# A retention layer and a rational feed-forward network in one kernel: fewer steps per weight, one transfer of constants, another opening order, and loads held back four deep

## The chip, the cores and the metric

The kernel runs on one core of a Trainium2 chip. The core has five engines with queues of their own: TensorE (PE in the rows, with PEld for its weight loads), VectorE (DVE), ScalarE (ACT), GpSimd (POOL) and SyncE (SP), which here only issues transfers. The metric is the device time of one execution in microseconds: the median of three runs.

## The reference

```python
# attention: 8 batches x 8 heads, 576 tokens, 64 dimensions a head
scores = q @ k^T / sqrt(64)
gamma  = 1 - 2 ** (-5 - head)
ret    = scores * where(i >= j, gamma ** (i - j), 0)
x      = (ret @ v), heads side by side          # 4608 tokens x 512
# feed-forward with a rational activation
h = x @ w_in                                    # 512 -> 2048
P = a0 + a1*h + a2*h^2 + a3*h^3
Q = 1 + |b0|*|h| + |b1|*h^2
out = (P / (Q + 1e-6)) @ w_out                  # 2048 -> 512
```

`w_in` and `w_out` come to the kernel as 64-bit floats and are turned into 32-bit ones on the chip.

## The kernel before

**Work.** The 4608 tokens are 36 units of 128. A unit brings two transfers of 512 KB, `qk` (q and k) and `kv` (k and v in another layout). The first eight units are handled by `attention`: q is scaled (`scale_q`), v is scaled (`scale_v`), PE makes the scores in `ps`, DVE masks them (`decay`), PE multiplies by v and adds to the state (`outputs`), PE adds what older tokens give through the state `S_sb` (`cross`), ACT and DVE split the result into `xhi` and `xlo` (`keep_hi`, `keep_lo`), DVE adds to the state (`grow`) and POOL fades it (`fade`). `ps` has two buffers, so the scores of a unit wait until the unit two places before has left its buffer; `cross` of a unit waits for `fade` of the one before. Later units go through `late_visit`, whose work lies between the steps of the feed-forward network.

**Feed-forward.** The tokens are 9 blocks of 512; each block has 16 steps, one for each 128 of the 2048 hidden columns. A step is `gemm1` (12 matmuls into `h`: high times high, high times low, low times high), a chain of elementwise work on ACT, DVE and POOL that leaves `g`, and `gemm2` (12 matmuls into `acc`). The first 24 steps are "early": they keep work in the PSUM bank of `h`.

**Weights.** Each of 32 weight tiles (512 KB of 64-bit words, `bits`) is turned into two 32-bit parts `w`. ACT takes the upper word without its sign (`begin`, tile `c`) and the next digits of the lower word (`digit`, tile `t`), DVE joins them by a shift and an or (`join`), DVE puts the sign back (`sign`), ACT rounds to the high part (`high_part`), POOL or DVE subtracts for the low part (`low_part`).

**What sets the order.** `Plan` holds every task with a due time and a cost, walks a clock of its own and writes each engine's instructions in the order in which it picks them; the engines then run strictly in that order and wait for each other by semaphores. `DUE`, `FIRST`, `HOLD`, `LAG`, `BACK`, `SLACK` and `LOADS` are the tables that steer it. `LOADS` lists the first transfers in order ("0" is a unit, "w0" a weight). All transfers are issued by SP. Their semaphores are eight, used in turn, so a transfer waits for the landing of the one eight places ahead.

**Start.** PE runs eight matmuls on zeros (`WARM`, into `unread`), then waits for the first scaled q.

Every instruction of a task passes through one wrapper, so nearly all rows of the profile carry its line (L71); the tiles tell them apart.

Of the kernel before, what the change touches and what calls it, by code (L numbers as in the profile page):

```python
# [34 lines left out]
V_POOL = range(4)  # L35
IN_BANK = 24
WARM = 8
AHEAD = -6
REACH = 7.4
FIRST = (-30.37, -29.34, -25.59, -24.33, -24.08, -16.98, -16.13, -17.66)  # L40
UNITS = (20.48, 2.58, -2.5)
LATE = {'scale': -1.0, 'decay': 0.201, 'middle': 0.3, 'grow': 0.524, 'fade': 0.6, 'keep_hi': 0.3, 'keep_lo': 0.5}
LEAD = -2.2
CNV = 3
CNT = 1
SHIFT = 60
LOADS = 'w0 0 gq mask 1 w1 gv 2 w2 3 w4 w5 w3 5 4 ab w7 6 w9 w6 w10 w8 7 w11'.split()
# [6 lines left out]
LAG = {'PE': 0.25, 'ACT': 0.097, 'DVE': 0.217, 'POOL': 0.16, 'SP': 0}  # L54
BACK = {'PE': 0.281, 'ACT': 0.157, 'DVE': 0.06, 'POOL': 0.097, 'SP': 0.015}
DUE = {'p_begin': 0.5, 'size': 0.727, 'p_mul': 0.7, 'p_mul2': 0.93, 'v_line': 0.797, 'v_mul': 0.806, 'log': 1.578, 'exp': 1.838, 'quot': 1.6, 'check': 1.65, 'better': 0.79, 'g_hi': 1.888, 'g_lo': 2.167, 'gemm2': 3.44, 'begin': -0.243, 'digit': 0.045, 'join': 0.128, 'sign': -0.303, 'high_part': 1.252, 'low_part': 0.8, 'scale_q': -0.354, 'scale_v': -0.5, 'scores': 0.178, 'decay': 0.311, 'outputs': 1.268, 'cross': 0.51, 'keep_hi': 1.415, 'keep_lo': 0.942, 'grow': 0.669, 'fade': 0.87}
HOLD = {('POOL', 'scale_v'): 3.0, ('DVE', 'p_begin'): 0.616, ('DVE', 'high_part'): 0.5, ('DVE', 'g_hi'): 1.221, ('DVE', 'keep_hi'): 1.153, ('DVE', 'g_lo'): 99.0, ('DVE', 'low_part'): 1.002, ('POOL', 'v_mul'): 0.229}
SLACK = {'PE': 0.19, 'ACT': 0.283, 'DVE': 0.2, 'POOL': 0.006, 'SP': 0.301}

ADJ = {}  # L60


class InOrder:
# [5 lines left out]
    def __getattr__(self, name):  # L69
        method = getattr(self.engine, name)  # L70
        return lambda *a, **k: self.tc.keep_in_program_order(method(*a, **k))  # L71

# [28 lines left out]
class Plan:  # L101
# [19 lines left out]
    def run(self):  # L121
# [14 lines left out]
        dma, left, now, reach = 0.0, len(self.tasks), -2.0, REACH  # L136
        while left:
            best = None
            for e, queue in wait.items():
                found = []  # L140
                for t in queue:
                    if e != "SP" and t.due > now + reach:
                        continue
                    names = [r for r, _ in t.takes]
                    ready = [self.rings[r].ready(names[:j].count(r)) for j, r in enumerate(names)]
                    if None in ready:
                        continue
                    _, _, shared, hold = t.ways[e]
                    s = max([0.0, *ready, *(a.end - BACK[e] * (a.engine == e) for a in t.after)]) + hold
                    s = max(s, clock[e])  # L150
                    if shared:
                        s = max(s, port["POOL" if e == "DVE" else "DVE"])
                    found.append((s, t.due, t))
# [21 lines left out]
            if e == "SP":  # L175
                clock["SP"] = s + 0.43
                dma = max(dma, s + 1.4) + cost
                t.end = dma + 1.0
# [15 lines left out]
def retention_ffn(ctx: ExitStack, tc: tile.TileContext, qk, kv, w_in, w_out, ab, masks, masks2, gq, gv, out):  # L194
# [8 lines left out]
    cnt = ctx.enter_context(tc.tile_pool(name="cnt", bufs=CNT))  # L203
# [9 lines left out]
    pe, act, dve, pool, sp = (InOrder(tc, e) for e in (nc.tensor, nc.scalar, nc.vector, nc.gpsimd, nc.sync))  # L213
# [3 lines left out]
        "qk": 2, "kv": 2, "xp": 2, "cnv": CNV, "t": CNT, "v": 2, "u": 2, "p": 3, "g": 3, "o0": 1, "o1": 1,  # L217
# [40 lines left out]
    bits, parts, joins = {}, {}, []  # L258
# [3 lines left out]
    def weight(order, s, w, f, loaded):  # L262
# [11 lines left out]
        def digit():  # L274
# [3 lines left out]
        def join():  # L278
# [20 lines left out]
        def low_part_v():  # L299
# [3 lines left out]
        t = add("ACT", d + DUE["begin"], 0.55, begin, [loaded], [("cnv", k)])  # L303
        t = add("ACT", d + DUE["digit"], 0.55, digit, [t], [("t", k)])
        t = add("DVE", d + DUE["join"], 0.61, join, [t], [], [("t", k)], True)
        joins.append(t)
        t = add("DVE", d + DUE["sign"], 0.61, sign, [t], shared=True)
        hi = add("ACT", d + DUE["high_part"], 0.53, high_part, [t], other=[("DVE", 0.5, high_part_v, True)])
        w_ready[k] = hi, add(
            "POOL", d + DUE["low_part"], 1.21, low_part, [hi], [], [("cnv", k)], True, [("DVE", 0.61, low_part_v, True)]  # L310
# [20 lines left out]
    def load_unit(n, due, after=()):  # L331
# [4 lines left out]
        def of(w, nm):  # L336
# [12 lines left out]
            add("SP", due + 0.01 * w, 524 / 390.0, of(w, nm), after, [] if late else [(nm, n)])  # L349
# [9 lines left out]
    def scale(n, at_, got, consts):  # L359
        def scale_q():  # L360
            q, _ = qk_of(n)
            pool.tensor_tensor(q, q, gq_sb, ALU.mult)

        def scale_v(by=dve):
            _, v = kv_of(n)
            dec = gv_sb[:, (n >= EARLY) * H : (n >= EARLY) * H + H].unsqueeze(2).broadcast_to([P, H, D])
            by.tensor_tensor(v, v, dec, ALU.mult)

        def scale_v_p():
            scale_v(pool)  # L370

        tq = add("POOL", at_(DUE["scale_q"]), 1.21, scale_q, [got[0], consts["gq"]], shared=True)
        tv = add("DVE", at_(DUE["scale_v"]), 0.6, scale_v, [got[1], consts["gv"]], shared=True,
                 other=[("POOL", 1.21, scale_v_p, True)])
        return tq, tv

    def attention(n, d, gap, got, consts, prev):
# [121 lines left out]
        th = add("ACT", at_(DUE["keep_hi"]), 0.5, keep_hi, done, [("xp", b)] if n % 4 == 0 else [], gives,  # L499
# [27 lines left out]
    def visit(n):  # L527
        m, heads = n + 1, [(j, g) for j in range(2) for g in range(NPAIR)]
        if "ps" not in late_s:
# [5 lines left out]
        if m < NU:  # L535
            bank["s"] = ps_h.tile([P, 512], F32, tag="h", name=f"ps{n}")
# [15 lines left out]
        if n >= EARLY:  # L552
# [17 lines left out]
    def decay(n):  # L570
        scr[n] = cnv.tile([P, 2, NPAIR, D], F32, tag="c", name=f"s{n}")
# [52 lines left out]
    def late_visit(n, d, got, consts, prev, hold):  # L624

        old, m = n >= EARLY, n + 1
        new, u = m < NU, (n + 1) % 9
        tq = tv = None
        if new:
            dn = d + LATE["scale"]  # L630
            tq = add("POOL", dn, 1.21, lambda: pool.tensor_tensor(qk_of(m)[0], qk_of(m)[0], gq_sb, ALU.mult),
# [7 lines left out]
            def scale_v_p():  # L639
# [3 lines left out]
                     other=[("POOL", 1.21, scale_v_p, True)])  # L643
        key = f"ps{n}"
        tm = te = None
        if m in sooner:
            tm = add("DVE", d - 1.5, 0.42, named(middle, m), [prev["visit"], prev.get("fade")])
        if n + 2 in sooner:
# [36 lines left out]
        if tm is None:  # L685
            tm = add("DVE", d + LATE["middle"], 0.42, named(middle, m), [ts, prev.get("fade"), *hold])
        tg = tf = None
        if u not in (4, 8):
            first = S_of[m + 1] == "S1" and "S1" not in S_of[: m + 1]
            tg = add("DVE", d + LATE["grow"], 0.42, named(grow, m), [tm, ts, *(joins if first else [])],  # L690
                     [("t", "S1")] if first else [])
        if u != 8:
            tf = add("POOL", d + LATE["fade"], 0.57, named(fade, m), [tg or tm], shared=True)
# [7 lines left out]
    def feed_forward(i, b, f, begins, ends):  # L701
        key = b, f
        early = i < IN_BANK
# [19 lines left out]
        def p_begin():  # L723
            e = els[key] = {"p": el3.tile([P, 512], F32, tag="p", name=f"p{nm}")}
            act.activation(e["p"], hs[key], AF.Identity, bias=a2, scale=a3)

        def p_begin_v():
            e = els[key] = {"p": el3.tile([P, 512], F32, tag="p", name=f"p{nm}")}
            dve.tensor_scalar(e["p"], hs[key], a3, a2, ALU.mult, ALU.add)
# [7 lines left out]
        def p_mul():  # L737
            p = els[key]["p"]
            dve.tensor_tensor(p, p, hs[key], ALU.mult)
# [279 lines left out]
```

## Time and profile before

| | |
|---|---|
| median of 3 runs | 899.9 us (898.13 to 900.02) |
| the profiled execution | 900.45 us, its span 898.6 us |
| PE busy | 882.8 us, 98% of the span |
| DVE, ACT, POOL busy | 790.4, 653.2, 163.7 us |
| transfers | 67.41 MB, 66.28 MB of them on SP's queue |
| chain that ended last | PE 92% |

PE is busy for all but 16 us of the span. In the table the busy times say how much of the span an engine worked, not that it was the bound; where PE waits, and for what, is in the rows below.

### The profile page before, as it was taken

How to read it: one execution, taken by the hardware profiler on the slowest of the kernel's cores; microseconds unless marked ns; L12 is line 12 of the kernel's file. 1: busy time of each engine (PE TensorE's matmuls, PEld its weight loads, DVE VectorE, ACT ScalarE, POOL GpSimd, SP SyncE). 2: the span in 40 equal slices, each digit the busy share in tenths (PEclk: the TensorE clock that was granted, in tenths of full speed). 3: DMA queues.
4: the chain of work that ended last, by engine and by line, in shares of the span. 5: the costliest groups of instructions: out<-in, count | busy, mean ns of one | idle time of the engine just before them, and what ended most of it. 6: DMA issues, size and time to landing. Idle time of an engine off the chain costs nothing.

```text
span 898.6 us, 17725 instructions
## 1 busy us (share of the span) xinstructions
PE 882.8 (98%) x7344; PEld 730.3 (81%) x7344; DVE 790.4 (88%) x1215; ACT 653.2 (73%) x1019; POOL 163.7 (18%) x141
## 2 busy tenths in 40 slices
PE   6999999999999999999999999999999999999998
PEld 5777888887888888888888888888888888888886
DVE  4899999988999888988989888988888888987976
ACT  3589999965667767666766677767676786767765
POOL 3565664522211100011101110001100001000000
PEclk9999999999999999999999999999999999999999
DMA  9991000033311112111211131112211021001001
GB/s 357 407 406 69 1 1 1 0 112 123 109 49 61 58 34 70 41 47 60 95 48 48 59 107 48 48 47 74 80 48 47 26 74 44 1 1 47 1 1 47
DMA packets 22641, 67.41 MB, mean 75 GB/s; under 512 B 2592, under 2 KB 4512, under 8 KB 22560
## 3 DMA queue, kind: packets, MB, share of 16 engines
q1 hardware_dynamic: 22560, 66.28, 20.6%
q8 instruction: 57, 0.93, 0.4%
q14 instruction: 24, 0.20, 0.1%
HBM read 56.83 MB, written 9.44 MB: 74 GB/s over the span
## 4 chain that ended last, share of the span: by engine, by line
PE 92%; DVE 3%; DMA 3%; issue 0%; SPq 0%; ACT 0%; POOL 0%; ACTq 0%; DVEq 0%; POOLq 0%
PE acc L71 42%; PE h L71 42%; PE ps L71 7%; DMA bits<-in_w_in 2%; DVE p L71 1%; DMA kv<-in_kv 1%; SPq L71 0%; DVE c L71 0%; DVE s L71 0%; DVE kv L71 0%; DVE xlo L71 0%; DVE v L71 0%; ACT xhi L71 0%; ACT o L71 0%; DVE g L71 0%
## 5 line engine op out<-in xcount | busy, mean ns | idle before, releaser
L71 PE MATMUL acc<-w,g 128*128 128x512 f32 x1632 | 394.2, 390 | 0.0
L71 PEld LDWEIGHTS acc<-w,g 128*128 128x128 f32 x1632 | 305.5, 188 | 64.2 <-POOL w L71 0.4
L71 PE MATMUL h<-xhi,w 128*128 128x512 f32 x1152 | 310.6, 392 | 0.8 <-DVE p L71 0.7
L71 PEld LDWEIGHTS h<-xhi,w 128*128 128x128 f32 x1152 | 213.9, 188 | 47.4 <-DVE p L71 2.1
L71 ACT ACTIVATE p<-h,ab_sb 128x512 f32<-128x512 f32 x143 | 110.8, 775 | 90.7 <-PE h L71 88.5
L71 PE MATMUL h<-xlo,w 128*128 128x512 f32 x576 | 154.2, 390 | 0.0
L71 DVE TENSOR_TENSOR p<-p,h 128x512 f32<-128x512 f32 x144 | 98.4, 683 | 53.8 <-ACT u L71 50.9
L71 DVE SCALAR_TENSOR_TENSOR p<-p,ab_sb,h 128x512 f32<-128x512 f32 x168 | 124.5, 744 | 10.6 <-ACT u L71 8.0
L71 PEld LDWEIGHTS h<-xlo,w 128*128 128x128 f32 x576 | 108.1, 188 | 23.0
L71 ACT ACTIVATE g<-p 128x512 fp32r<-128x512 f32 x136 | 85.6, 629 | 46.5 <-DVE p L71 44.3
L71 ACT ACTIVATE u<-v,qc 128x512 f32<-128x512 f32 x120 | 86.7, 723 | 44.4 <-DVE v L71 44.4
L71 ACT ACTIVATE v<-u,absb 128x512 f32<-128x512 f32 x124 | 101.1, 815 | 3.6
L71 DVE SCALAR_TENSOR_TENSOR p<-p,ab_sb,u 128x512 f32<-128x512 f32 x120 | 95.7, 798 | 4.3 <-ACT u L71 4.3
L71 ACT ACTIVATE u<-h 128x512 f32<-128x512 f32 x144 | 84.8, 589 | 10.5 <-DVE v L71 5.7
L71 DVE SCALAR_TENSOR_TENSOR p<-v,p 128x512 f32<-128x512 f32 x120 | 86.4, 720 | 3.9
L71 DVE TENSOR_TENSOR v<-v,u 128x512 f32<-128x512 f32 x120 | 83.1, 693 | 4.3 <-ACT v L71 3.2
L71 DVE SCALAR_TENSOR_TENSOR v<-v,u 128x512 f32<-128x512 f32 x120 | 84.6, 705 | 0.0
L71 DVE TENSOR_TENSOR g<-p,g 128x512 fp32r<-128x512 f32 x112 | 77.3, 690 | 3.8 <-ACT g L71 2.9
L71 ACT ACTIVATE u<-u 128x512 f32<-128x512 f32 x120 | 75.0, 625 | 2.1
L71 POOL TENSOR_TENSOR qk<-qk,gq_sb 128x512 f32<-128x512 f32 x36 | 49.4, 1374 | 84.6 <-DMA qk<-in_qk 75.9
L71 PEld LDWEIGHTS ps<-qk 64*64 64x64 f32 (+1 forms) x1024 | 38.0, 146 | 18.8 <-issue 10.4
L71 POOL TENSOR_TENSOR S_sb<-S_sb,gv_sb 128x256 f32<-128x256 f32 x18 | 15.7, 872 | 191.7 <-DVE S_sb L71 190.0
(58 smaller groups left out, 766.3 us busy)
## 6 DMA issues: line engine op xcount, KB each, us to landing
qk<-in_qk SPq DMA_DIRECT2D x36, 512.0 KB, 3.9
kv<-in_kv SPq DMA_DIRECT2D x36, 512.0 KB, 5.2
bits<-in_w_in SPq DMA_DIRECT2D x16, 512.0 KB, 10.1
bits<-in_w_out SPq DMA_DIRECT2D x16, 512.0 KB, 10.2
out<-o SPq DMA_DIRECT2D x14, 512.0 KB, 3.3
out<-o SPq DMA_DIRECT2D x8, 256.0 KB, 2.3
x<-in_kv SPq DMA_DIRECT2D x7, 256.0 KB, 5.1
gq_sb<-in_gq SPq DMA_DIRECT2D x1, 256.0 KB, 6.5
```

Source lines behind the costliest of these rows:

```text
L71: return lambda *a, **k: self.tc.keep_in_program_order(method(*a, **k))
```

## The change

- `begin` now uses the parametric rectifier in place of the absolute value: positive words keep their scale, negative ones are multiplied by minus 2 to the 32, which sets the bit that `join`'s shift moves to the sign's place. `sign` goes. `begin` and `digit` write in place in `bits`, so tile `t` goes, and `join` writes `c`.
- Four constants (`gq`, `gv`, the second mask, `ab`) come in one tile `fac`, 301 KB, in the first transfer; the second mask is no longer loaded later.
- In early steps three additions of a per-partition constant move from ACT to DVE instructions that were there anyway (`p_begin` to `p_mul`, `v_line` to `v_mul`), and the logarithm's bias is a number in the instruction.
- `v_mul` runs on POOL in nine steps (0 to 5, 10, 11, 17) instead of four.
- The planner's tables are new: load order, due times of the early steps (`DUE`; later steps keep the old ones as `STEADY`), costs, holds; `scale_q` may go to DVE. It also knows the rule below.
- Each transfer from the fifth to the 46th waits for the landing of the one four places ahead (`Loads`). There are eleven warm-up matmuls instead of eight.
- `late_visit` can now also serve units below eight (`DENSE`, `VISITS`); with `DENSE = 8` it doesn't.

```diff
-WARM = 8
+WARM = 11
-LOADS = 'w0 0 gq mask 1 w1 gv 2 w2 3 w4 w5 w3 5 4 ab w7 6 w9 w6 w10 w8 7 w11'.split()
+LOADS = 'gq 0 mask 1 0v 2 1v 2v 3 w0 5 3v 5v w2 w1 w5 4 w4 6 w3 w6 4v w9 w7 w11 w10 7v 7 6v w8'.split()
+OUTSTANDING = 8
+THROTTLE = 4
+THROTTLED = 46
...
+class Loads(InOrder):
+    def dma_start(self, *a, **k):
+        new = self.tc.keep_in_program_order(self.engine.dma_start(*a, **k))
+        if THROTTLE <= len(self.begun) < THROTTLED:
+            after = mybir.DependencyInfo(mybir.DependencyClass.Sync, mybir.DependencyReason.DATA)
+            self.tc.add_manual_dep(new.ins, self.begun[-THROTTLE].ins.name, after, reason="few loads at a time")
+        self.begun.append(new)
+        return new
...
         def begin():
-            c_[0] = cnv.tile([P, DM], I32, tag="c", name=f"c{nm}")
-            act.activation(c_[0].bitcast(F32), words()[1].bitcast(F32), AF.Abs, scale=math.ldexp(1.0, -112))
+            x = words()[1].bitcast(F32)
+            act.activation(x, x, AF.Prelu, scale=math.ldexp(1.0, -112), alpha=-math.ldexp(1.0, 32))
 
         def digit():
-            c_[1] = cnt.tile([P, DM], I32, tag="t", name=f"t{nm}")
-            act.activation(c_[1], words()[2], AF.Copy, scale=15 * 2.0**-17)
+            act.activation(words()[0], words()[2], AF.Copy, scale=15 * 2.0**-17)
 
         def join():
-            dve.scalar_tensor_tensor(c_[0], c_[0], 3, c_[1], ALU.logical_shift_left, ALU.bitwise_or)
-
-        def sign():
-            dve.scalar_tensor_tensor(c_[0], words()[1], -0x80000000, c_[0], ALU.bitwise_and, ALU.bitwise_or)
+            c_[0] = cnv.tile([P, DM], I32, tag="c", name=f"c{nm}")
+            dve.scalar_tensor_tensor(c_[0], words()[1], 3, words()[0], ALU.logical_shift_left, ALU.bitwise_or)
...
-            act.activation(e["p"], hs[key], AF.Identity, bias=a2, scale=a3)
+            if early:
+                act.activation(e["p"], hs[key], AF.Copy, scale=a3)
+            else:
+                act.activation(e["p"], hs[key], AF.Identity, bias=a2, scale=a3)
...
-            act.activation(e["r"], e["v"], AF.Ln, bias=qc)
+            act.activation(e["r"], e["v"], AF.Ln, bias=QC)
```

SP's queue at its start, before. `qk` and `kv` carry the unit's number, `bits0_f` is tile f of `w_in`.

```order
L71 DMA bits0_0_117<-in_w_in 128x512
L71 DMA qk0_119<-in_qk 128x1024
L71 DMA kv0_121<-in_kv 128x1024
L71 DMA gq_sb_101<-in_gq 128x512
L71 DMA mask_sb_98<-in_masks 128x320
L71 DMA qk1_125<-in_qk 128x1024
L71 DMA kv1_127<-in_kv 128x1024
L71 DMA bits0_1_129<-in_w_in 128x512
L71 DMA gv_sb_100<-in_gv 128x20
```

The same place in the change:

```order
L90 DMA fac_99<-in_factors 128x602
L90 DMA qk0_116<-in_qk 128x1024
L90 DMA mask_sb_98<-in_masks 128x320
L90 DMA qk1_119<-in_qk 128x1024
L90 DMA kv0_122<-in_kv 128x1024
L90 DMA qk2_124<-in_qk 128x1024
L90 DMA kv1_127<-in_kv 128x1024
L90 DMA kv2_138<-in_kv 128x1024
L90 DMA qk3_143<-in_qk 128x1024
L90 DMA bits0_0_171<-in_w_in 128x512
```

Constants and `qk0` are now the first two; the first weight goes from place 1 to 10; `kv1` stays at place 7.

DVE's queue at its start, before (`s` is the masked scores, `S_sb` the state, `kv0<-kv0` the scaling of v):

```order
L71 SCALAR_TENSOR_TENSOR c0_0_132<-c0_0_132,t0_0_136 128x512
L71 SCALAR_TENSOR_TENSOR c0_0_132<-bits0_0_117,c0_0_132 128x512
L71 TENSOR_TENSOR w0_0_152<-c0_0_132,w0_0_152 128x512
L71 TENSOR_TENSOR s0_179<-ps0_164,mask_sb_98 128x1024
L71 TENSOR_TENSOR kv0_121<-kv0_121,gv_sb_100 128x512
L71 TENSOR_TENSOR kv1_127<-kv1_127,gv_sb_100 128x512
L71 TENSOR_TENSOR s1_226<-ps1_183,mask_sb_98 128x1024
L71 COPY S_sb_105<-ps0_164 128x256
L71 TENSOR_TENSOR kv2_138<-kv2_138,gv_sb_100 128x512
L71 TENSOR_TENSOR xlo0_252<-ps0_164,xhi0_251 128x4x128
L71 SCALAR_TENSOR_TENSOR c0_1_198<-c0_1_198,t0_1_205 128x512
L71 SCALAR_TENSOR_TENSOR c0_1_198<-bits0_1_129,c0_1_198 128x512
```

The same place in the change:

```order
L79 TENSOR_TENSOR s0_140<-ps0_129,mask_sb_98 128x1024
L79 TENSOR_TENSOR kv0_122<-kv0_122,fac_99 128x512
L79 TENSOR_TENSOR s1_174<-ps1_145,mask_sb_98 128x1024
L79 TENSOR_TENSOR kv1_127<-kv1_127,fac_99 128x512
L79 COPY S_sb_101<-ps0_129 128x256
L79 TENSOR_TENSOR xlo0_180<-ps0_129,xhi0_179 128x4x128
L79 TENSOR_TENSOR kv2_138<-kv2_138,fac_99 128x512
L79 TENSOR_TENSOR S_sb_101<-S_sb_101,ps1_145 128x256
L79 TENSOR_TENSOR xlo0_180<-ps1_145,xhi0_179 128x4x128
L79 TENSOR_TENSOR s2_232<-ps2_215,mask_sb_98 128x1024
L79 SCALAR_TENSOR_TENSOR c0_0_243<-bits0_0_171 128x512
```

The weights' work has moved behind the attention of units 0 and 1, and is one instruction a weight instead of two.

PE's queue between the first units and the first `gemm1` (`h0_0`), in the change:

```order
L79 MATMUL ps1_145<-qk1_119,S_sb_101 64x128 x8
L79 MATMUL ps2_215<-qk2_124 128x128 x8
L79 MATMUL ps3_234<-qk3_143 128x128 x8
L79 MATMUL ps2_215<-s2_232,kv2_138 64x128 x8
L79 MATMUL ps2_215<-kv2_138 64x64 x8
L79 MATMUL ps2_215<-qk2_124,S_sb_101 64x128 x8
L79 MATMUL ps3_234<-s3_263,kv3_200 64x128 x8
L79 MATMUL ps3_234<-kv3_200 64x64 x8
L79 MATMUL ps3_234<-qk3_143,S_sb_101 64x128 x8
L79 MATMUL ps5_325<-qk5_176 128x128 x8
L79 MATMUL h0_0_348<-xhi0_179,w0_0_266 128x512 x4
```

Before, the same eleven rows stand there in the same order; PE's queue differs up to here only in the three added warm-up matmuls.

## Rows read from the trace of the kernel before

**Rows 1.** Windows: stretch, length, busy (instructions) by engine, clock, DMA share, GB/s

```profile
0.00:30.86 30.86, 21.03 (x272) 19.12 (x272) 18.18 (x26) 11.48 (x18) 11.69 (x14) 1.00 0.96 370
30.86:62.00 31.14, 30.38 (x312) 24.41 (x311) 28.98 (x43) 22.43 (x39) 17.43 (x17) 1.00 1.03 407
62.00:112.00 50.00, 49.91 (x219) 40.35 (x218) 48.57 (x76) 49.63 (x86) 29.69 (x23) 1.00 0.19 75
112.00:894.40 782.40, 781.52 (x6547) 646.41 (x6545) 694.62 (x1073) 568.69 (x879) 104.90 (x89) 1.00 0.15 49
894.40:898.60 4.20, 0.00 (x0) 0.00 (x0) 0.00 (x0) 0.92 (x2) 0.00 (x0) 0.80 0.65 246
```

**Rows 2.** Timeline of PE, 0 to 31 us: start, duration, what, idle before

```profile
1.06 3.78 PE L71 MATMUL unread<-S_sb 128*128 128x128 f32 x16 [1.06 <-DVE qc L71]
10.04 3.79 PE L71 MATMUL ps<-qk 64*128 64x128 f32 x32 [5.20 <-POOL qk L71]
...
16.48 1.04 PE L71 MATMUL ps<-s,kv 128*64 128x128 f32 x16
17.36 0.63 PE L71 MATMUL ps<-kv 128*64 128x64 f32 x16
18.88 1.09 PE L71 MATMUL ps<-qk,S_sb 64*64 64x128 f32 x16 [0.89 <-POOL S_sb L71]
19.90 1.16 PE L71 MATMUL ps<-qk 64*128 64x128 f32 x16
...
30.86 1.20 PE L71 MATMUL h<-xhi,w 128*128 128x512 f32 x4
```

**Rows 3.** Timeline of SP's issues, 0 to 12 us

```profile
0.74 0.38 SPq L71 DMA_DIRECT2D bits<-in_w_in  x1
...
7.95 0.33 SPq L71 DMA_DIRECT2D kv<-in_kv  x1
...
11.61 0.33 SPq L71 DMA_DIRECT2D bits<-in_w_out  x1
```

**Rows 4.** Timeline of ACT, 0 to 17 us

```profile
4.38 0.66 ACT L71 ACTIVATE c<-bits 128x512 f32<-128x512 f32 x1 [2.36 <-DMA bits<-in_w_in]
...
16.70 0.60 ACT L71 ACTIVATE xhi<-ps 128x512 fp32r<-128x512 f32 x1 [2.59 <-PE ps L71]
```

**Rows 5.** Timeline of POOL, 8 to 18 us

```profile
8.73 1.26 POOL L71 TENSOR_TENSOR qk<-qk,gq_sb 128x512 f32<-128x512 f32 x1 [8.28 <-DMA gq_sb<-in_gq]
...
17.84 0.99 POOL L71 TENSOR_TENSOR S_sb<-S_sb,gv_sb 128x256 f32<-128x256 f32 x1 [2.11 <-DVE S_sb L71]
```

**Rows 6.** Timeline of DVE, 12 to 19 us

```profile
12.17 1.23 DVE L71 TENSOR_TENSOR s<-ps,mask_sb 128x1024 f32<-128x1024 f32 x1 [3.68 <-PE ps L71]
...
17.33 0.42 DVE L71 COPY S_sb<-ps 128x256 f32<-128x256 f32 x1 [1.60 <-ACT xhi L71]
17.68 0.68 DVE L71 TENSOR_TENSOR kv<-kv,gv_sb 128x512 f32<-128x512 f32 x1
...
18.88 1.73 DVE L71 SCALAR_TENSOR_TENSOR c<-c,t 128x512 int32<-128x512 int32 x1
```

**Rows 7.** The weights' tile by form: count, duration min/median/max in ns, first and last start

```profile
L71 ACT ACTIVATE c<-bits x32: 652/667/712, 4.4 to 175.4; 128x512 f32<-128x512 f32 x32
L71 DVE SCALAR_TENSOR_TENSOR c<-bits,c x32: 678/686/1127, 6.3 to 180.3; 128x512 int32<-128x512 int32 x32
```

**Rows 8.** The page's costliest groups: busy us, mean ns of one, idle before

```profile
L71 ACT ACTIVATE u<-v,qc 128x512 f32<-128x512 f32 x120 | 86.7, 723 | 44.4 <-DVE v L71 44.4
...
L71 ACT ACTIVATE u<-u 128x512 f32<-128x512 f32 x120 | 75.0, 625 | 2.1
```

**Rows 9.** The page's transfers by tile: count, size, median us from issue to landing

```profile
qk<-in_qk SPq DMA_DIRECT2D x36, 512.0 KB, 3.9
...
bits<-in_w_in SPq DMA_DIRECT2D x16, 512.0 KB, 10.1
```

**Rows 10.** Chain that ended last, 90 to 97 us: start, duration, what

```profile
93.52 2.72 PE acc L71 x12
```

More of the change, by code (lines that the diff above doesn't have):

```diff
@@ L57 @@
-HOLD = {('POOL', 'scale_v'): 3.0, ('DVE', 'p_begin'): 0.616, ('DVE', 'high_part'): 0.5, ('DVE', 'g_hi'): 1.221, ('DVE', 'keep_hi'): 1.153, ('DVE', 'g_lo'): 99.0, ('DVE', 'low_part'): 1.002, ('POOL', 'v_mul'): 0.229}
+LAG = {'PE': 0.21, 'ACT': 0.138, 'DVE': 0.118, 'POOL': 0.08, 'SP': 0}
+BACK = {'PE': 0.21, 'ACT': 0.0, 'DVE': 0.0, 'POOL': 0.0, 'SP': 0.0}
+ENTER = {'PE': 0.03, 'ACT': 0.0, 'DVE': 0.0, 'POOL': 0.045, 'SP': 0.0}
+PORT = 0.33
+FETCH = ((4.8, 1.0), (15.5, 1.1))
+DUE = {'p_begin': -0.998, 'size': 1.908, 'p_mul': -0.347, 'p_mul2': 5.296, 'v_line': 1.475, 'v_mul': 1.541, 'log': 3.284, 'exp': -0.985, 'quot': 1.963, 'check': 2.017, 'better': -1.338, 'g_hi': 1.445, 'g_lo': -1.676, 'gemm2': 4.596, 'begin': -0.512, 'digit': 1.055, 'join': -0.091, 'high_part': 1.387, 'low_part': 6.778, 'scale_q': 0.308, 'scale_v': 1.347, 'scores': 2.952, 'decay': 0.786, 'outputs': 6.305, 'cross': -5.06, 'keep_hi': -5.352, 'keep_lo': 3.008, 'grow': -0.794, 'fade': 1.051}
@@ L148, in run @@
                     _, _, shared, hold = t.ways[e]
-                    s = max([0.0, *ready, *(a.end - BACK[e] * (a.engine == e) for a in t.after)]) + hold
-                    s = max(s, clock[e])
+                    s = max([0.0, *ready, *(a.end + (-BACK[e] if a.engine == e else ENTER[e]) for a in t.after)]) + hold
+                    s = max(s, clock[e], landed[-(THROTTLE if len(landed) - OUTSTANDING < THROTTLED else OUTSTANDING)] if e == "SP" else 0.0)
                     if shared:
-                        s = max(s, port["POOL" if e == "DVE" else "DVE"])
+                        held = port["POOL" if e == "DVE" else "DVE"]
+                        s = held + PORT * (e == "DVE") if held > s else s
                     found.append((s, t.due, t))
@@ L175, in run @@
             if e == "SP":
-                clock["SP"] = s + 0.43
-                dma = max(dma, s + 1.4) + cost
-                t.end = dma + 1.0
+                clock["SP"] = s + 0.47
+                fetch = sum(x for at, x in FETCH if dma < at <= max(dma, s + 1.5) + cost)
+                dma = max(dma, s + 1.5) + cost + fetch
+                t.end = dma + 0.8
+                landed.append(t.end)
             else:
@@ L302, in weight @@
         d = min(s - LEAD, AHEAD + order)
[L303 to L308, printed above, removed]
+        t = add("ACT", d + DUE["begin"], 0.56, begin, [loaded])
+        t = add("ACT", d + DUE["digit"], 0.56, digit, [t])
+        t = add("DVE", d + DUE["join"], 0.6, join, [t], [("cnv", k)], shared=True)
+        hi = add("ACT", d + DUE["high_part"], 0.52, high_part, [t], other=[("DVE", 0.5, high_part_v, True)])
         w_ready[k] = hi, add(
-            "POOL", d + DUE["low_part"], 1.21, low_part, [hi], [], [("cnv", k)], True, [("DVE", 0.61, low_part_v, True)]
+            "POOL", d + DUE["low_part"], 1.25, low_part, [hi], [], [("cnv", k)], True, [("DVE", 0.6, low_part_v, True)]
         )
@@ L348, in load_unit @@
         return [
-            add("SP", due + 0.01 * w, 524 / 390.0, of(w, nm), after, [] if late else [(nm, n)])
+            add("SP", due[w], 524 / 409.0, of(w, nm), after, [] if late else [(nm, n)])
             for w, nm in enumerate(("qk", "kv"))
@@ L702, in feed_forward @@
         key = b, f
+        due = DUE if i < IN_BANK else STEADY
         early = i < IN_BANK
```

223 lines of the change are left out of this document (124 added, 99 removed).

## Prediction

> **What bounds the kernel now.** I read the windows first, since an average over the span hides that the stages differ. From 112 us to the last matmul at 894.4 PE is busy 781.52 of 782.40 us, and from 62 to 112 it is busy 49.91 of 50 [rows 1]. There PE's own work is the bound: a faster ACT or DVE gives nothing, and every microsecond that PE's queue starts earlier is kept to the end. The 4.2 us after the last matmul are eviction and store, which the change leaves alone. So the time is decided in the first 62 us: 9.83 us without work up to 30.86, 0.76 from there to 62, and 0.97 from there to 894.4 [rows 1].
>
> The timeline of PE says where the first of these lie. PE warms up to 4.84, then waits 5.20 us for the first scaled q [rows 2]. POOL scaled it at 8.73, and waited 8.28 us for the table `gq` [rows 5], fourth in SP's queue behind a weight, `qk0` and `kv0`. The first scores then took 3.79 us for two units where one later took 1.16, so they ran at half the pace. `cross` of unit 1 starts at 18.88, and the first `gemm1` at 30.86 [rows 2]: 11.98 us, in which PE's rows are the same before and after the change. I use these two moments as posts.
>
> **When data land.** From 30.86 to 62 transfers run at 407 GB/s, 0.407 MB a microsecond [rows 1], so 512 KB (0.524 MB) take 1.29 us. Landings follow from who waits: ACT starts on the first transfer at 4.38 [rows 4]; SP issues the 11th at 7.95 when the third, `kv0`, is in, and the 15th at 11.61 when the seventh, `kv1`, is in [rows 3]. Bytes up to these three: 0.524, 1.573, 3.047 MB. From the first to the third 1.049 MB should take 2.58 us and took 3.57, so there is a hole of 1.0 us; from the third to the seventh 3.62 are due and 3.66 measured, so there is none.
>
> In the change `qk0` ends at 0.308 + 0.524 = 0.832 MB: it lands at 4.38 + 0.308/0.407 = 5.1 (6.1 if the hole comes before it). `qk1` ends at 1.520 MB, `kv0` at 2.045, `kv1` at 3.094. Counted back and on from 11.61 they land at 7.9, 9.15 and 11.7. `kv1` lands no sooner than before. Before, it lay ready until 16.48, when its matmuls began [rows 2], since the first q was late; now the data are the bound there.
>
> **The opening, step by step.** POOL scales `qk0` from 5.2 in 1.26 [rows 5], so the first scores start at 6.5 instead of 10.04. The three added warm-up matmuls cost 3.78/8 each [rows 2] and end at 1.06 + 11 x 0.47 = 6.3: hidden, by 0.2 us; if the data came sooner they would cost that. The second scores start at 7.9 + 1.26 = 9.2 and end at 10.4. `outputs` of unit 0 takes 1.51 (16.48 to 17.99) [rows 2], to 11.9; ACT splits in 0.60 [rows 4], DVE copies the state in 0.42 [rows 6] behind the scaling of `kv1` (0.68, from 11.75) [rows 6], POOL fades in 0.99 [rows 5]: 14.0. `outputs` of unit 1 starts at 12.5 and ends at 14.0. `cross` of unit 1 thus starts at 14.1 with a few hundredths of handover, instead of 18.88: 4.8 us earlier.
>
> This takes PE at full pace. At the pace of the row at 10.04 (1.9 for a unit's scores, twice 1.51 for outputs) the same sum is 9.2 + 1.9 + 3.0 + 0.6 + 0.42 + 0.99 = 16.1 and the gain 2.7. I take full pace: in the change PE works from 1.06 through the first scores with a gap of about 0.2 us, whereas before the slow rows followed a gap of 5.20. The granted clock reads 1.00, the 2.4 GHz level, over that whole stretch [rows 1], so the column does not show what halved the pace. The Trainium skill, "TensorE: Matmul & The Clock Gate", Part 1, says that the slow state is the default and that activity ends it. By it the slow rows were the 1.2 GHz level, the added warm-up helps, and the sum is the 4.8; by the column the slow pace has another cause and may stay, which gives the 2.7. The durations side with the page.
>
> From `cross` to the first `gemm1` I take the 11.98 as measured. DVE has three joins there instead of three pairs; 0.69 each [rows 7] makes up to 2.0 less if all lie on the path. `kv3`, now 12th (5.71 MB), lands at 18.2, or 19.2 with another hole; it is scaled behind the state's update of unit 2, some 7 us after `cross`, so it is in. First `gemm1`: 26.1.
>
> **The other parts.** `sign` goes: 32 x 0.686 = 22 us of DVE [rows 7], between 6 and 181 us. DVE is busy 48.57 of 50 from 62 to 112 while PE works 49.91 [rows 1], so this buys slack, not time. The rectifier is not in the trace. Bounds of that size: 0.625 and 0.723, an ACT row without and one with a pointer [rows 8], against the 0.667 of the instruction it replaces [rows 7]: -1.3 to 1.8 us of ACT over 32. I take 0, the nearest row. Writing in place costs nothing by the same rows, as they already step over every second word. The logarithm without its pointer should fall from 0.723 towards the 0.625 of the exponential [rows 8], 0.1 x 144 = 14 us of ACT, behind PE. The two copies in early steps that lose a pointer save about as much each, and DVE's instructions take the addition over. Five more `v_mul` on POOL, at 1.26 each by the nearest row [rows 5], are 6.3 us where POOL is busy 29.69 of 50 [rows 1]; what POOL and DVE then lose to each other shows in a join of 1.73 instead of 0.69 [rows 6, 7], 1.0 a clash, five at most: 5 us of DVE against the 22 it gains. Cover for all of these is PE's unbroken queue after 62; without it ACT would be first, busy 49.63 of 50 there [rows 1].
>
> **The throttle.** SP issues nothing but transfers, so behind its wait stand only later transfers. Four of 512 KB take 5.2 us on the wire; a transfer alone lands 3.9 us after issue [rows 9]. Four in flight cover that, with 1.3 us to spare, and the stream loses nothing; nor does it gain, since 10.1 us with eight in flight [rows 9] is 1.26 each, pure queue.
>
> **Sum.** Opening -4.8; the 1.73 us idle after the first `gemm1` stay; tail 0. The profiled execution, 900.45 with a span of 898.6, would be 895.65; it lies 0.55 above the median, so I forecast 899.9 - 4.8 = 895.1, its own range 893.1 (joins on the path) to 897.2 (slow pace).
>
> **Rivals.** *More than the opening* (0.20): the joins are on the path, and the slack on DVE and ACT also removes the idle 1.73: 895.1 - 2.0 - 1.7 = 891.4. For it: DVE is 93% busy from 30.86 to 62. Against: PE lost only 0.76 there [rows 1].
>
> *ACT takes the gain back* (0.12): PE comes 4.8 us earlier into the stage in which ACT had 0.37 us of 50 left, and half of the lead is lost there: 897.5. For it: 99% busy. Against: three cheaper ACT instructions a step, about 0.3 us, in some 9 steps (a step is twice 12 matmuls of 2.72 us [rows 10]), leave 2.8 us more.
>
> *The throttle makes holes, and the kernel is slower* (0.08): if a loaded round trip is not 3.9 but longer than 5.2, the pitch of the loads is a quarter of it. The 29th transfer is `kv6`, the last that the attention in the opening needs; at 1.29 it lands at 11.7 + 22 x 1.29 = 40.1, 41 with another hole, and PE reaches it after four `gemm1` (2.72 each [rows 10]), three scores (1.16), three outputs (1.51) and two `cross` (1.09) [rows 2], 21.1 in all, at 47.2. Counted without a gain that is 52.0, so with 0.8 for scaling it may land at 51.2: 10.2 late in 28 gaps, a pitch of 1.65, a round trip of 6.6. There the gain is gone; at 7.5 (1.88, 16.5 late) it is 6.3 slower: 906.2. For it: the 10.1; against: that this is eight times the wire. The Trainium skill, "DMA: Bandwidth & Descriptors", section "Bandwidth", wants transfers of 1 MiB and gives them 341 GB/s; with eight of half the size in flight the trace has 407. At 341 the pitch would be 1.54, `kv6` 7.0 late, and 1.6 of the gain lost.
>
> The remaining 0.04 is what I have not seen. My forecast has 0.56.
>
> **Chances.** 0.2%, 1.8 us, is about what can be told from no change here. Faster than 898.1: the forecast, the first rival, and some 0.07 of the second: 0.83. Within: 0.07. Slower: 0.10. The range runs from 891.4 to 899.3; above it lie the throttle and the rest.
>
> **What would show it.** Right: first scores near 6.5 and 1.2 us long, `cross` of unit 1 near 14.1, first `gemm1` near 26, loads at 407 GB/s with issues 1.3 apart, PE's idle time from there on under 2 us. Wrong: scores of 1.9 us; SP's steps over 1.5; idle PE between 26 and 112 behind ACT; a rectifier much over 0.67.

## The result: slower, and the profile after

The changed kernel takes 905.84 us (median of four runs, 905.38 to 907.0) against 899.64 (898.13 to 900.02) of the kernel before (its three earlier runs and one beside the change): ratio 1.0074, 95% interval 1.0057 to 1.0091. The forecast was 895.1 with a range up to 899.3. The profiled execution took 906.09 with a span of 904.1, 5.5 us more than before.

Windows of the changed kernel, columns as in [rows 1]:

```profile
0.00:27.30 27.30, 19.13 (x279) 17.23 (x279) 14.27 (x21) 8.57 (x15) 10.64 (x14) 1.00 0.92 340
0.00:30.86 30.86, 22.69 (x310) 20.04 (x312) 16.38 (x23) 11.36 (x19) 14.20 (x17) 1.00 0.92 338
30.86:62.00 31.14, 29.31 (x294) 23.50 (x289) 25.51 (x38) 27.65 (x48) 21.24 (x21) 1.00 0.96 355
62.00:112.00 50.00, 47.03 (x204) 37.63 (x204) 43.52 (x62) 45.30 (x79) 32.38 (x25) 1.00 0.32 128
112.00:182.00 70.00, 67.33 (x334) 55.66 (x334) 60.98 (x89) 62.55 (x112) 36.37 (x29) 1.00 0.00 1
182.00:240.00 58.00, 58.00 (x715) 47.81 (x711) 50.04 (x79) 34.32 (x58) 13.78 (x11) 0.97 0.29 97
240.00:899.90 659.90, 659.24 (x5510) 544.77 (x5508) 580.46 (x890) 454.60 (x705) 54.10 (x50) 1.00 0.15 50
```

Length less busy is PE's idle time. To 30.86 it is 8.17 us where it was 9.83; from there to 62, 1.83 for 0.76; from 62 on, 2.97 + 2.67 + 0.66 = 6.30, where [rows 1] gives 0.09 + 0.88 = 0.97. In all 4.74 more. PE's busy time adds 0.76, which makes up the 5.5. DVE and ACT, which had 1.43 and 0.37 us of 50 left in 62 to 112, now have 6.48 and 4.70: they work less and PE still waits. The loads run at 338 and 355 GB/s instead of 370 and 407.

Timeline of PE in the changed kernel, the opening [rows 2] and all its waits of over 0.3 us from 62 to 240:

```profile
1.06 4.30 PE L79 MATMUL unread<-S_sb 128*128 128x128 f32 x22 [1.06 <-DVE S_sb L79]
6.67 1.16 PE L79 MATMUL ps<-qk 64*128 64x128 f32 x16 [1.31 <-POOL qk L79]
...
13.40 1.09 PE L79 MATMUL ps<-s,kv 128*64 128x128 f32 x16 [1.65 <-DVE kv L79]
14.32 0.64 PE L79 MATMUL ps<-kv 128*64 128x64 f32 x16
14.88 1.09 PE L79 MATMUL ps<-qk,S_sb 64*64 64x128 f32 x16
...
27.30 1.19 PE L79 MATMUL h<-xhi,w 128*128 128x512 f32 x4
...
72.09 1.19 PE L79 MATMUL h<-xhi,w 128*128 128x512 f32 x4 [0.82 <-DVE p L79]
...
100.39 1.19 PE L79 MATMUL h<-xhi,w 128*128 128x512 f32 x4 [0.79 <-DVE p L79]
...
104.59 0.73 PE L79 MATMUL acc<-w,g 128*128 128x512 f32 x2 [1.19 <-ACT o L79]
...
181.63 0.93 PE L79 MATMUL ps<-kv 64*64 64x64 f32 x16 [2.67 <-DVE p L79]
182.48 4.33 PE L79 MATMUL acc<-w,g 128*128 128x512 f32 x12
```

The opening went about as forecast. The scores run at full pace, `cross` of unit 1 starts at 14.88 instead of 18.88, the first `gemm1` at 27.30 instead of 30.86. The new waits are behind elementwise work. The longest is that of the first late visit, which waits for the last early step's p; the twelve matmuls behind it took 4.33 instead of 2.72 us at a granted clock of 0.67.

What DVE and POOL did ahead of two of these waits. Timeline of DVE in the changed kernel, near 87 and 177 us:

```profile
87.13 4.09 DVE L79 SCALAR_TENSOR_TENSOR c<-bits 128x512 int32<-128x512 int32 x3
91.15 0.74 DVE L79 SCALAR_TENSOR_TENSOR p<-p,fac,h 128x512 f32<-128x512 f32 x1
...
176.99 1.79 DVE L79 TENSOR_TENSOR v<-v,u 128x512 f32<-128x512 f32 x1
```

Timeline of POOL there:

```profile
87.43 1.54 POOL L79 TENSOR_TENSOR g<-p,g 128x512 fp32r<-128x512 f32 x1 [6.19 <-ACT g L79]
89.08 3.31 POOL L79 TENSOR_TENSOR w<-c,w 128x512 fp32r<-128x512 f32 x2
...
176.95 1.29 POOL L79 TENSOR_TENSOR w<-c,w 128x512 fp32r<-128x512 f32 x1 [0.92 <-ACT w L79]
```

Three joins took 4.09 us instead of three times 0.68, while POOL subtracted for g and w; the `v_mul` at 176.99 took 1.79, and POOL had begun 0.04 earlier. Instructions that read h from PSUM (p<-p,fac,h) keep their 0.74. Counted over the median of their form, six of DVE's instructions between 62 and 182 lose 5.8 us in this way, five of them 1.1 each and one 0.4; before, four lost 1.2. POOL's part in the six is its subtractions for g and w and one scaling of v; none is a `v_mul` that the change put on POOL. The Trainium skill, "SBUF — State Buffer", section "SBUF: two separate sides", says why: VectorE and GpSimd share one pair of ports as an exclusive lock, a VectorE operation with two SBUF inputs needs it, and whoever starts first keeps it for the whole instruction. The rows agree: the 1.1 us come near one POOL instruction, 1.29 to 1.54, and DVE was always the one that began later.

The weights' tile by form in the changed kernel [rows 7]:

```profile
L79 ACT ACTIVATE bits<-bits x64: 647/666/697, 16.5 to 167.1; 128x512 f32<-128x512 f32 x32, 128x512 int32<-128x512 uint16 x32
L79 DVE SCALAR_TENSOR_TENSOR c<-bits x32: 675/684/1786, 18.8 to 178.7; 128x512 int32<-128x512 int32 x32
```

Half of the 64 instructions are the rectifier and half `digit`; none takes more than 0.697, and the median of 0.666 is what `begin` cost before, 0.667 [rows 7].

### The profile page after: what moved, and what is told of

Its sections match the earlier page's. It is cut to its first block, busy times and chain, and to the rows that moved or that the text cites. A ratio compares the mean times of both kernels' runs of the same rounds, so it can differ in the third digit from the quotient of the medians.

```text
span 904.1 us, 17711 instructions
## 1 busy us (share of the span) xinstructions
PE 883.6 (98%) x7350; PEld 729.4 (81%) x7350; DVE 776.9 (86%) x1175; ACT 636.8 (70%) x1017; POOL 172.1 (19%) x150
## 4 chain that ended last, share of the span: by engine, by line
PE 77%; DVE 9%; ACT 8%; DMA 4%; issue 1%; POOL 0%; ACTq 0%; SPq 0%; DVEq 0%
PE acc L79 36%; PE h L79 36%; PE ps L79 6%; DVE p L79 4%; ACT h L79 2%; ACT bits L79 2%; DVE c L79 2%; ACT u L79 1%; DMA bits<-in_w_in 1%; DVE v L79 1%; DMA qk<-in_qk 1%; ACT p L79 1%; DMA bits<-in_w_out 1%; DVE h L79 1%; ACT w L79 1%
## 5 line engine op out<-in xcount | busy, mean ns | idle before, releaser
L79 ACT ACTIVATE p<-h,fac 128x512 f32<-128x512 f32 x141 | 107.5, 763 | 102.5 <-PE h L79 101.4
L79 DVE SCALAR_TENSOR_TENSOR p<-p,fac,h 128x512 f32<-128x512 f32 x192 | 142.2, 744 | 20.4 <-ACT u L79 12.3
L79 DVE TENSOR_TENSOR p<-p,h 128x512 f32<-128x512 f32 x120 | 82.2, 685 | 43.7 <-ACT u L79 41.3
L79 ACT ACTIVATE v<-u,absb 128x512 f32<-128x512 f32 x129 | 105.3, 816 | 3.9
L79 ACT ACTIVATE u<-v 128x512 f32<-128x512 f32 x120 | 75.7, 631 | 40.7 <-DVE v L79 40.6
L79 DVE SCALAR_TENSOR_TENSOR p<-p,fac,u 128x512 f32<-128x512 f32 x120 | 92.8, 773 | 9.3 <-ACT u L79 5.4
L79 DVE SCALAR_TENSOR_TENSOR v<-v,u 128x512 f32<-128x512 f32 x120 | 89.4, 745 | 0.0
L79 DVE SCALAR_TENSOR_TENSOR p<-v,p 128x512 f32<-128x512 f32 x120 | 84.2, 702 | 3.4
L79 POOL TENSOR_TENSOR qk<-qk,fac 128x512 f32<-128x512 f32 x36 | 48.2, 1338 | 96.1 <-DMA qk<-in_qk 95.9
L79 POOL TENSOR_TENSOR S_sb<-S_sb,fac 128x256 f32<-128x256 f32 x18 | 14.6, 814 | 184.3 <-DVE S_sb L79 184.3
L79 PEld LDWEIGHTS ps<-qk 64*64 64x64 f32 (+1 forms) x1024 | 36.5, 141 | 16.1 <-issue 10.2
```

## The experiments

Each ratio is to the kernel before, timed beside it. Theory: the new order makes PE wait behind DVE and ACT. Rivals: the throttle; the new instructions themselves.

**1. No wait** (the changed kernel, order on every engine the same).

```diff
-        if THROTTLE <= len(self.begun) < THROTTLED:
+        if WAITED and THROTTLE <= len(self.begun) < THROTTLED:   # WAITED = False
```

> The changed kernel with the same order on every engine, but no transfer waits for the one four places ahead (only the eight semaphores limit them). Theory T (the throttle: with four in flight the stream had landing steps of 1.4 to 2.8 us about twelve times in the first 66 us, where the kernel before had two steps over 1.3, and the late data throw the planned order out of step until 182 us): landings 1.28 apart but for two holes, the 29th transfer (kv6) in before 43 instead of 44.57, no PE idle time behind DVE or ACT after 62 or much less than the 5.6 us of the change, time 896 to 900. Rival O (the order itself: ACT and DVE wait for each other in turn between 62 and 182 whatever the loads do): the loads get faster and the time stays within 1.5 us of 905.8.

903.81 us, ratio 1.006 (1.0039 to 1.0081). Loads are back at 408 GB/s in 31 to 62, PE's idle time to 62 is 8.1 us instead of 10.0. The time lies between the two forecasts. The waits after 62 stay, here the ones at 98 and at the visit (timeline of PE):

```profile
98.33 1.21 PE L80 MATMUL h<-xhi,w 128*128 128x512 f32 x4 [0.79 <-DVE p L80]
...
179.55 0.68 PE L80 MATMUL ps<-kv 64*64 64x64 f32 x16 [2.65 <-DVE p L80]
180.16 3.02 PE L80 MATMUL acc<-w,g 128*128 128x512 f32 x12
```

So late data are not their cause. The clock did not fall behind this wait of 2.65 (3.02 for the twelve), as it did behind 2.67 in the changed kernel; of the four timed runs two read 0.999 and took 902.4 and 902.7, two read 0.994 and 0.996 and took 906.9 and 904.9.

**2. The kernel before with the wait alone** (`Loads` added, nothing else).

> The kernel before with its own order on every engine, and only the wait added: each of the first 46 transfers waits for the landing of the one four places ahead. Theory T: the same extra holes appear, the stream ends 4 to 8 us later than 70.4, and the kernel is 3 to 7 us slower than 899.6. Rival O: holes or not, the time stays within 1.5 us of 899.6.

901.53 us, ratio 1.0027 (1.0016 to 1.0039): the throttle costs 2.4 us by itself, less than the theory's 3 to 7 and more than the rival's 1.5. First `gemm1` at 32.51. Part of it may be the clock, which reads below 1.00 in both windows. Windows, for comparison with [rows 1]:

```profile
0.00:30.86 30.86, 18.87 (x256) 17.00 (x256) 16.14 (x24) 9.99 (x16) 10.33 (x13) 0.89 0.88 302
30.86:62.00 31.14, 30.12 (x313) 24.18 (x314) 27.14 (x41) 20.93 (x36) 17.28 (x18) 0.95 0.96 343
```

**3. New instructions with the old tables** (`DUE`, `FIRST`, `HOLD`, `LAG`, load order and so on as before, no throttle).

> The changed kernel's instructions (rectifier, no sign step, constants in one transfer, additions moved to DVE in early steps, costs of the planner) under the due times, holds, load order, warm-up and V_POOL of the kernel before, without the wait. Theory O (order and wait are what cost, the instructions are cheaper): 896 to 900, first gemm1 near 31 as before and PE idle under 2 us after it. Rival I (the new instructions cost, for instance through the longer chain in early steps): ACT and DVE wait for each other after 62 as in the change, and the time is over 902.

912.69 us, ratio 1.0152 (1.0137 to 1.0167): over 902, as the rival had it, with one wait of 5.53 us for an eviction at 106.58 among others. But the old tables were made for the old instructions, so this doesn't tell whether the new ones or the order that the planner made of them cost the time.

**4. Old due times for the feed-forward chain** (14 of `DUE`, with the throttle).

```diff
+DUE.update(STEADY)
```

> The changed kernel with the wait, but the fourteen due times of the feed-forward chain in early steps (p_begin to gemm2) set back to those that later steps use; the rest of the new tables stays. Theory O, in the form that these due times make the order in which ACT and DVE wait for each other: the PE idle time of 5.6 us between 62 and 182 falls under 2 and the time to 899 to 902, with the opening as in the change (first gemm1 near 27.3). Theory T: the idle time stays, 904 to 908.

919.39 us, ratio 1.0224 (1.0207 to 1.024). A miss: PE's idle time from 62 to 240 grew to 12.4 us. Undoing part of a table plans the whole order anew; later experiments keep the order fixed and change one thing.

**5. The visit later.** No throttle; on PE the visit's second part stands behind the next twelve acc matmuls, all else in place.

```diff
+MATMUL acc<-w,g 128x512 (12)
 MATMUL ps<-qk, ps<-kv
-MATMUL acc<-w,g 128x512 (12)
```

> The changed kernel without the throttle's wait (its time without the wait: ratio 1.006 to before), and on TensorE one thing moved: the first late visit's second half stands behind the next sum of twelve acc matmuls instead of ahead of it; the order on the other four engines is the same, row for row. Theory 'place': TensorE's 2.65 us stall at 181 is a place in the queue, and the 1.6 us that the twelve sums lose at the lower clock behind it goes with it: idle in 112 to 182 from 2.65 to under 0.3, the sum of twelve back at 2.72 us, the time down by about 4.2 us, ratio to before about 1.001 (0.999 to 1.003). Rival 'elementwise bound': VectorE and ScalarE set the pace there, so the 2.65 us come back as another stall within 60 us; ratio stays 1.005 to 1.007.

903.47 us, ratio 1.005 (1.0038 to 1.0063): near nothing, as the rival had it. The wait moved to DVE's mask behind the visit (timeline of PE):

```profile
179.72 0.68 PE L81 MATMUL ps<-kv 64*64 64x64 f32 x16
181.98 0.32 PE L81 MATMUL ps<-qk 64*64 64x64 f32 x2 [1.58 <-DVE s L81]
```

**6. POOL waits where the plan had it behind DVE.** No throttle; order the same, but an operation of POOL that the planner marked as sharing the port and put right behind such an operation of DVE now waits for that one to end (up to about 185 us).

```diff
+                    if e == "POOL" and s < UNTIL and port["DVE"] > s - NEAR:   # 185.0, 0.4
+                        emit = self.behind(emit, shared_last)   # POOL after DVE's last shared one
```

> The changed kernel without the throttle's wait, with one kind of wait added up to about 185 us: where the planner had put one of GpSimd's two-input operations right behind one of VectorE's two-input operations, GpSimd now waits for that VectorE operation to end, so that it can't start ahead of it. Order on all engines is the same. Theory 'port': the joins of 1.75 us (six of VectorE's operations that lose 5.8 us in all between 62 and 182) lose it to a GpSimd operation that began a moment sooner than the order meant; with the wait their excess falls below 2.5 us, TensorE's stall at 98 (0.79 us) goes, and the ones at 102 (1.3 us) and at 180 (2.65 us) shrink by a half or more; ratio to before 1.002 to 1.004. Rival 'incidental': VectorE has over 6 us of idle time in each of these stretches and would only wait elsewhere, or GpSimd's results come later by as much; TensorE's idle after 62 stays at 5.5 to 6.5 us and the ratio at 1.005 to 1.007.

899.26 us, ratio 1.0001 (0.9992 to 1.0009). Adding waits made it faster, by the ratios (1.006 and 1.0001) some 5 us and more than was expected: of DVE's lengthened instructions between 62 and 182 one is left (0.5 us), and PE's waits at 98, 102 and 180 are gone, though this profiled execution also opened 2 us late (first `gemm1` at 28.7 instead of 26.6).

**7. Both** (5 and 6).

> Both of these edits in one kernel. If place and port both hold: no stall of over 1 us on TensorE between 62 and 240, ratio to before 0.998 to 1.001, with the opening's gain (2.4 us less idle before 31 than before) showing at last. If only place holds: 1.000 to 1.002, as with the first edit alone. If the elementwise engines are the bound: 1.004 or more.

899.42 us, ratio 1.0002 (0.9993 to 1.0011): POOL's waits alone do it, the visit's place does nothing.

**8. Six in flight** (the changed kernel, `THROTTLE = 6`).

> The changed kernel with its wait, six transfers in flight instead of four; order on every engine the same. Theory 'runs dry': each transfer is spread over 16 DMA engines, and with four in flight the engines that are ahead have nothing queued when one lags; with six the 54th transfer lands within 0.5 us of the kernel with no wait (against some 2 us later with four), and the ratio to before is that of no wait, 1.005 to 1.006. Rival 'the wait itself' (SyncE's queue pays for each of the 42 waits, whatever their depth): the loads are as late as with four, ratio 1.007.

905.55 us, ratio 1.0077 (1.0065 to 1.0089). At first sight the wait itself costs. But the 46th transfer landed at 62.8, as with no wait (63.0; 68.6 with four); instead the opening ran slowly. Timeline of PE, and the window of 10 to 15 us:

```profile
7.46 1.16 PE L79 MATMUL ps<-qk 64*128 64x128 f32 x16 [1.72 <-POOL qk L79]
9.46 2.08 PE L79 MATMUL ps<-qk 64*128 64x128 f32 x16 [0.84 <-POOL qk L79]
```

```profile
10.00:15.00 5.00, 5.00 (x58) 4.78 (x56) 2.33 (x4) 0.60 (x1) 1.26 (x1) 0.50 1.03 418
```

The granted clock is 0.50, the 1.2 GHz level, and the second scores take 2.08 instead of 1.16. The clock read 0.50 again for 3.4 us behind the wait at the visit, where the twelve matmuls took 4.59. PE had idled 1.72 us ahead of the first scores, 1.88 in experiment 6 where the opening's clock fell too, and 1.08 to 1.31 where it did not. All five timed runs have a mean clock of 0.993 to 0.996. In experiment 6 the runs fall in two groups: 897.8 to 898.3 at a clock of 0.999 and up, 899.1 to 900.5 below.

**9. Longer warm-up** (experiment 6 with `WARM` 14 instead of 11).

> The kernel with the added GpSimd waits and no throttle (ratio 1.0001), with fourteen warm-up matmuls instead of eleven and nothing else moved. In the profiles so far the granted clock fell to about half between 5 and 15 us where TensorE had stood idle 1.72 us or more ahead of the first scores (1.88 with this order, 1.72 with six in flight), and stayed full where it had stood 1.08 to 1.31 us. Theory 'idle ahead of the scores': the longer warm-up leaves at most 0.9 us of idle, the clock is 1.00 in 5 to 15 in every run, first gemm1 near 26.8 us instead of 28.7, and the time is that of the faster half of the earlier runs, 897.8 to 898.5, ratio to before 0.9975 to 0.9995. Rival 'the scores are late for their load and the clock is no matter': ratio 0.9992 to 1.001 as before, spread of 2 us and more between runs.

898.13 us, ratio 0.9992 (0.9983 to 1.0001). Half confirmed: 5 to 15 us is at full clock in the profile and seven runs of eleven have a mean clock of 0.999 or more (four of eleven in experiment 6), but in the others the clock still falls, in the profiled one between 20 and 30 us (0.81 and 0.85), and its first `gemm1` came at 28.3, not 26.8. The interval overlaps that of experiment 6: that the longer warm-up gains time is not shown.

**10. The same with the throttle at four.**

> The same with the throttle's wait put back, four in flight: only that wait differs. Theory 'shallow queue': transfers late by 5 to 6 us at the 46th (68.6 against 63 us), TensorE's idle before 62 about 1.9 us longer, ratio 0.0015 to 0.003 above the kernel without it. Rival 'covered': the idle of the elementwise engines (15 us between 62 and 182) takes up what is late; the two ratios agree within 0.0008.

899.31 us, ratio 1.0007 (0.9998 to 1.0015): 1.2 us more than without, at the lower end of what the theory gave; the 46th transfer landed at 66.4 instead of 63.4, 3 us late and not 5 to 6. The intervals overlap; taken with experiment 2 the throttle costs some 1 to 2.5 us. This kernel is the changed one plus POOL's waits and three warm-up matmuls, and these take back 0.0067 of the 0.0074.

**11. The same with six.**

> The same with the wait at six in flight. With six and the shorter warm-up the transfers were as early as with none (46th at 62.8 us), yet the ratio was 1.0077 with a clock of 0.50 in 10 to 15 us. If that came from the opening's clock alone: the ratio agrees with that of no wait within 0.0008. If the waiting itself costs on SyncE: 0.0015 to 0.003 above it.

897.99 us, ratio 0.9994 (0.9986 to 1.0003), as without a wait: the loss in experiment 8 was not SP's waiting. Its trace leaves the clock, in the opening (first `gemm1` at 28.6, against 26.3 here) and behind the visit's wait. Transfers of `bits` by tile, in 0 to 70 us (median us to landing), with four (experiment 10), six and eight in flight (experiment 9):

```profile
bits<-in_w_in SPq DMA_DIRECT2D x16, 512.0 KB, 5.5
```

```profile
bits<-in_w_in SPq DMA_DIRECT2D x16, 512.0 KB, 7.8
```

```profile
bits<-in_w_in SPq DMA_DIRECT2D x16, 512.0 KB, 10.2
```

A quarter of 5.5 is 1.38, a sixth of 7.8 is 1.30, an eighth of 10.2 is 1.28: of these depths four is too few. This profiled execution opens at full clock, and the joins, POOL behind them and the visit without a wait read so (timelines of DVE, POOL and PE):

```profile
84.55 1.88 DVE L83 SCALAR_TENSOR_TENSOR c<-bits 128x512 int32<-128x512 int32 x3
```

```profile
86.58 1.30 POOL L83 TENSOR_TENSOR g<-p,g 128x512 fp32r<-128x512 f32 x1 [7.07 <-DVE c L83]
87.84 2.56 POOL L83 TENSOR_TENSOR w<-c,w 128x512 fp32r<-128x512 f32 x2
```

```profile
173.36 1.15 PE L83 MATMUL ps<-qk 64*64 64x64 f32 x32
174.54 0.68 PE L83 MATMUL ps<-kv 64*64 64x64 f32 x16
```

POOL's three operations end at 90.4, 5.85 us after the joins begin; in the changed kernel they ended at 92.4, 5.3 after. POOL loses half a microsecond there, DVE gains 2.2.

**12. Two of POOL's waits only** (experiment 6 with the waits planned between 60 and 90).

> The changed kernel without the throttle, warm-up of eleven, and just two of the added GpSimd waits: ahead of two of its subtractions for g (near 71 and 85 us), which there began a moment ahead of VectorE's joins. If these joins (3.25 us of excess in three) are what sets the rest off: TensorE's stalls at 98 and 102 go, idle in 62 to 112 about 1.1 us, the stall at 180 shrinks to 0.5 to 1.6 (another collision, 1.1 us at 175, stays), ratio 1.001 to 1.003. If it takes all of the added waits: ratio above 1.004 and 2.6 us of idle at 180.

902.41 us, ratio 1.0037 (1.0025 to 1.0049). Timelines of DVE and PE:

```profile
84.34 1.89 DVE L83 SCALAR_TENSOR_TENSOR c<-bits 128x512 int32<-128x512 int32 x3
...
172.27 1.79 DVE L83 TENSOR_TENSOR v<-v,u 128x512 f32<-128x512 f32 x1
```

```profile
176.91 0.68 PE L83 MATMUL ps<-kv 64*64 64x64 f32 x16 [2.66 <-DVE p L83]
```

The two waits free the three joins, and PE's idle time from 62 to 112 falls from 2.95 to 0.94, its waits at 98 and 102 with it. The clash at 172 and the wait at the visit stay. So the clashes ahead of a wait make it. The ratio lies between the two forecasts (up to 1.003, above 1.004). The wait at the visit did not shrink as expected (2.66, not 0.5 to 1.6): PE gained at 98 and 102 and came sooner to a p that the clash at 172 still delays.

## Why the prediction was wrong, point by point

**The cover that failed.** "Cover for all of these is PE's unbroken queue after 62": this step decides the miss. In the sum it is the term "the 1.73 us idle after the first `gemm1` stay"; measured are 8.13, of which 6.30 lie after 62. The prediction saw the clash and priced it well (1.0 each; measured 1.1), but weighed it as 5 us against the 22 that DVE gains. That its "five at most" comes near the six of the trace is luck: it counted the five `v_mul` that go to POOL, and the six clashes are with other work of POOL. And slack counted over a stage does not help a chain whose next member is due now. The chain of work that ended last, in the changed kernel, runs through the three joins at 87, which its view merges into the row below. Thirteen us further on PE's h waits for a `better` of DVE, and `acc` behind it for an eviction by ACT:

```profile
87.22 4.01 DVE c L79 x3
```

The engines did less and PE's queue broke all the same. Experiments 6 and 11 show it, and 12 for a part: with POOL held back, the order unchanged, the loss goes. The prediction put idle PE behind ACT under its rival "ACT takes the gain back", as an engine running out of time; the engine had 4.70 us left.

**The throttle.** "Four in flight cover that ... and the stream loses nothing" failed too: 1.2 to 2.4 us. The sum took four times the wire, 5.2, against a lone transfer's 3.9. Measured with four in flight: 5.4 to 5.5, and 355 GB/s in 31 to 62 us against 407 [rows 1]. The rival "holes" named the mechanism and took `kv6` as its post; it landed at 44.6, not at 41, but before the 51 at which the rival put the loss of the whole gain. That rival's worst case, 906.2, is near the measured time by luck: it stood on a round trip of 7.5, and the throttle is the smaller part of the loss. Why the steps lengthen was not settled: four and six in flight tell the depth, not what each of the 16 DMA engines did.

**The opening.** The mechanism was right (6.67 for 6.5, 14.88 for 14.1, 27.30 for 26.1), and the first `gemm1` came 3.56 us earlier of the 4.8 forecast. "From `cross` to the first `gemm1` I take the 11.98 as measured" held, with 12.4. PE's work ahead of the first `gemm1` is the same but for the added warm-up, so the 3.56 split into 1.66 of idle time (9.83 to 8.17) and 1.90 of busy time (21.03 [rows 1] to 19.13), which is pace, after what the longer warm-up takes. The warm-up was mis-sized: six more instructions (three matmuls) took 0.52 us and not 1.4, so PE stood idle 1.31 ahead of the first scores and not 0.2; full pace came all the same. The gain was lost behind the post: 1.07 more idle time to 62, 5.33 more after it, and 2.66 more busy time, 1.6 of them in the twelve matmuls at a clock of 0.67; the rest was not traced further. With early loads and a full clock the idle time to 31 falls by 3.1 (9.83 to 6.72, experiment 11), and the first `gemm1` comes at 26.3.

The Trainium skill, "TensorE: Matmul & The Clock Gate", Part 1, on which the prediction leaned for full pace, was borne out there: in experiment 8 the pace is half and the granted clock reads 0.50. The column that spoke against the page [rows 1] had no reading to give: the trace of the kernel before holds no record of the clock ahead of 16.26 us (the changed kernel's begin at 4.40), and a stretch without a record is printed as 1.00. Where the records begin, the pace changes: `outputs` of unit 0 has this row, twice the one at 16.48 [rows 2].

```profile
14.05 1.97 PE L71 MATMUL ps<-s,kv 128*64 128x128 f32 x16 [0.22 <-DVE kv L71]
```

**The base.** The sum was made from 899.9. Over the later runs the kernel before has medians of 898.9 to 899.2, so 0.7 to 1.0 of the forecast gain may lie in the choice of the base.

**Rectifier, in-place writing, logarithm, `sign`:** right; 0.666 for 0.667, `digit` among them, and they do buy slack.

**The best version** is that of experiment 11 or 9: 0.8% faster than the changed kernel, 1 us below the kernel before by the medians, with intervals that just take in 1 (0.9983 to 1.0001). The profiled spans differ by more, 895.5 against 898.6; the profiled execution before is slow for its kernel, whose later runs have spans of 897.1 to 897.4 in the median.

## What to carry to other kernels

Slack in a stage is no cover for a chain that is in order on each engine: look where the next instruction waits, and ask of every pair of engines that can block each other which one starts first if the plan's clock is off by half a microsecond. A semaphore that fixes the meant order can be faster than none. Measure an opening by the moment of an instruction ahead of which the work is the same, and split what is gained into idle time and pace; idle time alone left out 1.90 of 3.56 us here. Before a clock of 1.00 is believed, look whether the rows keep the pace that goes with it. Where transfers in flight are limited, leave a margin over the sum: six were as good as no limit here, four were not.

## What was not expected of the hardware

- A DVE join that starts 0.10 to 0.36 us after a POOL subtraction, or a `v_mul` 0.04 after one, takes 1.75 to 1.79 instead of 0.68; waiting for three joins set POOL back by 0.6.
- The granted clock fell to 0.50 in the opening after 1.72, 1.88 and (experiment 10) 2.07 us without work ahead of the first scores, not after 1.08 to 1.31, and in experiment 7 not after 1.92 ahead of the second scores; and behind 2.65 us without work at 180 it stayed at 1.00 in one execution and read 0.67 behind 2.67 in another.
- With four transfers of 512 KB in flight the stream is slower than with eight by 7% in the landing times (1.38 against 1.28 us each) and by 13% in the changed kernel's window of 31 to 62 us (355 against 407 GB/s; 389 in experiment 10).
